# VectorE's exponential: an addition and a product as one scalar-tensor-tensor instruction

## The chip, the cores and the metric

One core of one Trainium2 chip. The metric is the device time of one execution in microseconds (us). The kernel before takes 2081.48 us, the median of three runs (2080.36 to 2085.64).

## The reference

Four residual layers on a sequence of 2048 tokens with 512 features, 32 heads of 16 each. Layers 0 and 2 are of kind A, layers 1 and 3 of kind B.

```python
# A: attention within each of 4 segments of 512 tokens, plus a memory M, z of the segments before
logits = einsum(q, k) * scale + mask          # mask: causal, within the segment
a_dot = softmax(logits) @ v
a_mem = (phi(q) @ M) / (phi(q) @ z + 1e-6)    # phi(t) = t + 1 where t > 0, else exp(t)
o = g * a_mem + (1 - g) * a_dot               # g = sigmoid(beta), per head
M, z = M + phi(k)^T v, z + sum(phi(k))
# B: full attention, 2048 x 2048 for each head, no mask
p = softmax(einsum(q, k) * Dh ** -0.5)
o = p @ v
# the program
x = x + A(layernorm(x)); x = x + B(layernorm(x)); x = x + A(layernorm(x)); x = x + B(layernorm(x))
```

The bulk of the work is the exponential of the scores: in each B layer 32 x 2048 x 2048 of them.

## The kernel before

**Banks and rounds.** Scores are made in pieces called banks: for one head, 128 keys on the partitions and up to 512 queries along the free dimension, which fills one of PSUM's eight banks with fp32. A group is one head and 512 queries; in a B layer it mostly has 64 banks (16 blocks of keys in each of four rows of TensorE). The program goes in rounds (`unit`). In each round TensorE (PE) makes three banks of scores into PSUM banks 0 to 2 or, every other round, 3 to 5. Then ScalarE (ACT) takes the exponential of all three in one instruction, 128 x 1536, PSUM to the SBUF tile `pT` (L1168). Two rounds later (three for A) PE multiplies `pT` with the values `VB` and adds it up in PSUM bank 6, which holds the group that is being summed. When a group ends, `finish` has VectorE (DVE) transpose that bank into `tT` (L1228) and take the reciprocal of the sums (L1232); GpSimd (POOL) multiplies the two (L1243). PE's first product of the next group waits for that transpose.

**The second exponential.** DVE takes some banks off ACT. `dx_pick` decides in each round whether one more bank of a B group is made, into PSUM bank 7; it looks at how far DVE is behind in the planner's account, at the time when bank 7 comes free, and at how many banks the group has given already. `dx_first` has DVE read the bank at once (L850): it scales it by a constant and writes it as a fixed-point number, 32 bits, into one of four buffers (`dxt` 0 and 1, later also the places of `KA` and `QA`). The upper 16 bits are the whole part of the exponent, the lower 16 the fraction. Two banks make a pair of 128 x 1024; sometimes a bank goes alone, 128 x 512. `dx_chain` then takes a pair through six instructions, each a step of its own: the fraction as an f16 `f` (L876), a first polynomial step `z` (L879), a product (L882), an addition (L884), a product (L886), and at last the whole part times 128 plus `z`, as an int16 whose bits are the bf16 result (L888). `f` and the result lie in one of five output buffers (`dxo`, and a part of `VA`), `z` in `dxz` or a part of `VA`. Two chains (`task_dx`) run at a time, and their steps alternate. PE multiplies the result with `VB` like any `pT`, at the earliest two rounds after the last step was put in (`dxq`).

**The order.** All instructions are put in order beforehand, by a planner that is part of the program: `Sched` keeps an estimated clock for each engine from the `ns` of each instruction (an instruction behind a busy engine adds `ns` less 85), and derives the semaphore waits. Each engine runs its instructions strictly in that order. Besides the attention there are background tasks: layer norms, projections, the memory of A, the output products, and the two chains. After every round `credit` gives a task budget for DVE (`cr_dve`, 1560 a round once all buffers are in use), and `background` runs steps as long as the budget covers the third value of a step's `yield`, the charge. `c` are the charges and `ns` the durations of the chain: 350, 610, 1150 and 690, 430, 1225 for a pair. Where `late("dve")`, DVE's clock less PE's, is over a limit, no step is run and no bank is taken. `keep_busy` adds products of zeros on PE until a round has a set number of columns.

The banks that A and B read and the tasks' needs decide which rounds count as low (few banks are ready); then no bank is taken.

Of the kernel before, what the change touches and what calls it, by code (L numbers as in the profile page):

```python
# [5 lines left out]
ALU = mybir.AluOpType  # L6
# [13 lines left out]
EXP_C1, EXP_C2, EXP_C3 = 128 * 0.69511679, 128 * 0.22764497, 128 * 0.07706706  # L20
# [222 lines left out]
class Builder:  # L243
# [621 lines left out]
    def dx_chain(self, k, b, ents, slot):  # L865


        w = 512 * len(ents)
        ns = (690, 430, 1225) if len(ents) == 2 else (420, 295, 690)
        half = self.dx_space("in", b).bitcast(dt.uint16).rearrange("p (n two) -> p two n", two=2)  # L870
        lo, hi = half[:, 0, 0:w], half[:, 1, 0:w]
        out = self.dx_space("out", slot)
        f, z, ob = out.bitcast(dt.float16)[:, 0:w], self.dx_space("z", k)[:, 0:w], out.bitcast(dt.int16)[:, 0:w]
        bt, bo, bz = self.b_dxt[b], [self.b_dxo[slot]], [self.b_dxz[k]]
        c = (350, 610, 1150) if self.wide else (440, 710, 1230)
        self.op("dve", lambda e: e.tensor_scalar(f, lo, 2.0 ** -16, None, op0=ALU.mult), reads=bt,  # L876
                writes=self.dx_writes("out", slot, self.b_dxo[slot]), ns=ns[0])
        yield [], 0, c[0]
        self.op("dve", lambda e: e.tensor_scalar(z, f, EXP_C3, EXP_C2, op0=ALU.mult, op1=ALU.add), reads=bo,  # L879
                writes=self.dx_writes("z", k, self.b_dxz[k]), ns=ns[1])  # L880
        yield [], 0, c[1]
        self.op("dve", lambda e: e.tensor_tensor(z, z, f, ALU.mult), reads=bo + bz, writes=bz, ns=ns[0])  # L882
        yield [], 0, c[0]
        self.op("dve", lambda e: e.tensor_scalar(z, z, EXP_C1, None, op0=ALU.add), reads=bz, writes=bz, ns=ns[1])  # L884
        yield [], 0, c[1]
        self.op("dve", lambda e: e.tensor_tensor(z, z, f, ALU.mult), reads=bo + bz, writes=bz, ns=ns[0])  # L886
        yield [], 0, c[2]
        self.op("dve", lambda e: e.scalar_tensor_tensor(ob, hi, 128.0, z, op0=ALU.mult, op1=ALU.add), reads=bt + bz, writes=bo, ns=ns[2])  # L888
        self.dx_bufs.append(b)
        self.dx_now[k] = []  # L890
        self.dx_use[slot] = len(ents)
        for i, (g, what, r) in enumerate(ents):
            self.dxq.append((self.step + 2, g, what, r, slot, i))
# [523 lines left out]
```

## Time and profile before

| | us |
|---|---|
| median of three runs | 2081.48 |
| the profiled execution | 2084.59 |
| its span | 2082.9 |
| ACT, all exponentials of scores (L1168), 1569 instructions | 1962.5 |
| DVE, first step of the taken banks (L850), 428 instructions | 291.2 |
| DVE, additions of the chain (L884) of 1024 | 86.8 |
| DVE, products of the chain (L886) of 1024 | 140.8 |
| DVE, last steps (L888) of 1024 | 247.3 |

The profiled execution is one run with the hardware profiler on. Its span runs from the first instruction to the last; 1.7 us of its time lie around it. PE is TensorE's products, PEld its weight loads, SP the queue that starts the transfers. A group's line gives the source line, the engine, the operation, the tile written and the tiles read, the shapes, the number of instructions, then the busy time, the mean duration of one in ns, and the idle time of the engine just before. Neighbours on DVE overlap, so the sum of durations is above the busy time of the engine. The TensorE clock granted was 0.978 of full speed.

### The profile page before, as it was taken

How to read it: one execution, taken by the hardware profiler on the slowest of the kernel's cores; microseconds unless marked ns; L12 is line 12 of the kernel's file. 1: busy time of each engine (PE TensorE's matmuls, PEld its weight loads, DVE VectorE, ACT ScalarE, POOL GpSimd, SP SyncE). 2: the span in 40 equal slices, each digit the busy share in tenths (PEclk: the TensorE clock that was granted, in tenths of full speed). 3: DMA queues.
4: the chain of work that ended last, by engine and by line, in shares of the span. 5: the costliest groups of instructions: out<-in, count | busy, mean ns of one | idle time of the engine just before them, and what ended most of it. 6: DMA issues, size and time to landing. Idle time of an engine off the chain costs nothing.

```text
span 2082.9 us, 35052 instructions
## 1 busy us (share of the span) xinstructions
PE 1787.6 (86%) x13708; PEld 494.1 (24%) x13708; DVE 1656.6 (80%) x3039; ACT 1990.0 (96%) x1610; POOL 383.9 (18%) x766
## 2 busy tenths in 40 slices
PE   7888899878988988889888888888888888888887
PEld 3222222222222222222222222222222222222222
DVE  6665655499568895898858986549999999999996
ACT  7788998999999999999999999999999999999998
POOL 4521433020060001500024001401100000000000
PEclk9898999999999999999999999999999999999999
DMA  4111100000000000000000001000000000000000
GB/s 143 21 21 21 20 5 19 11 1 14 9 1 11 1 14 9 11 11 1 14 16 4 1 1 21 11 11 1 11 1 1 1 11 1 1 1 11 1 1 11
DMA packets 67142, 24.81 MB, mean 12 GB/s; under 512 B 59808, under 2 KB 66464, under 8 KB 66976
## 3 DMA queue, kind: packets, MB, share of 16 engines
q1 hardware_dynamic: 66976, 22.57, 4.9%
q8 instruction: 107, 1.75, 0.4%
q14 instruction: 59, 0.48, 0.1%
HBM read 6.30 MB, written 2.10 MB: 4 GB/s over the span
## 4 chain that ended last, share of the span: by engine, by line
ACT 41%; PE 20%; DVE 19%; issue 15%; POOL 1%; DMA 1%; SPq 1%; ACTq 0%; DVEq 0%
ACT pT L1168 41%; PE ps L372 20%; DVE dxo L888 2%; DVE tT L1228 2%; DVE dxt L850 1%; POOL pT L1183 1%; DVE dxo L876 1%; DVE KA L850 1%; DVE x L769 1%; DVE VA L882 1%; DVE QA L850 1%; DVE dxz L886 1%; DVE dxz L882 1%; DVE VB L388 1%; DVE KB L388 1%
## 5 line engine op out<-in xcount | busy, mean ns | idle before, releaser
L1168 ACT ACTIVATE pT<-ps 128x1536 bf16<-128x1536 f32 (+2 forms) x1569 | 1962.5, 1511 | 66.1 <-PE ps L372 54.1
L372 PE MATMUL ps<-qm,KB 32*128 32x512 bf16 x4096 | 507.1, 386 | 174.5 <-ACT pT L1168 164.3
L372 PE MATMUL ps<-wB,zero 128*17 128x512 bf16 x2072 | 632.8, 388 | 0.0
L372 PE MATMUL ps<-pT,VB 128*17 128x512 bf16 x3668 | 495.7, 387 | 23.4 <-DVE tT L1228 14.5
L1243 POOL TENSOR_TENSOR ob<-tT,rd 128x256 bf16<-128x256 f32 x127 | 92.4, 727 | 1143.6 <-DVE rd L1232 1112.6
L372 PEld LDWEIGHTS ps<-qm,KB 32*128 32x128 bf16 x4096 | 126.1, 91 | 708.2 <-ACT pT L1168 616.6
L1183 POOL TENSOR_SCALAR_AFFINE_SELECT pT<-pT 128x384 bf16<-128x384 bf16 (+2 forms) x512 | 210.5, 427 | 332.8 <-ACT pT L1168 323.2
L372 PEld LDWEIGHTS ps<-wB,zero 128*17 128x17 bf16 x2072 | 177.6, 92 | 112.8 <-issue 6.6
L372 PEld LDWEIGHTS ps<-pT,VB 128*17 128x17 bf16 x3668 | 114.3, 87 | 354.5 <-issue 299.5
L850 DVE TENSOR_SCALAR dxt<-ps 128x512 uint32<-128x512 f32 x213 | 145.1, 681 | 20.7 <-PE ps L372 19.7
L1228 DVE STREAM_TRANSPOSE tT<-ps 128x512 f32<-128x512 f32 x112 | 79.6, 710 | 66.5 <-PE ps L372 64.7
L372 PE MATMUL ps<-qm,KA 32*128 32x384 bf16 (+3 forms) x1024 | 104.6, 318 | 30.1 <-ACT pT L1168 27.3
L372 PE MATMUL ps<-dxo,VB 128*17 128x512 bf16 x343 | 130.0, 386 | 0.1
L372 PE MATMUL ps<-pT,VA 128*17 128x384 bf16 (+3 forms) x1024 | 103.5, 321 | 20.4 <-DVE tT L1228 14.3
L1086 POOL TENSOR_SCALAR qm<-QB,par 128x512 bf16<-128x512 bf16 x84 | 79.9, 958 | 192.5 <-PE ps L372 190.6
L372 PE MATMUL ps<-xT,wB 128*128 128x512 bf16 x256 | 73.2, 390 | 10.8 <-DVE KB L388 3.0
L850 DVE TENSOR_SCALAR KA<-ps 128x512 uint32<-128x512 f32 x109 | 74.1, 680 | 8.2 <-PE ps L372 7.7
L850 DVE TENSOR_SCALAR QA<-ps 128x512 uint32<-128x512 f32 x106 | 72.0, 680 | 4.2 <-PE ps L372 4.0
L372 PE MATMUL ps<-xT,wA 128*128 128x512 bf16 x256 | 70.4, 385 | 5.2 <-DVE xT L525 0.9
L769 DVE TENSOR_TENSOR x<-x,ps 128x512 bf16<-128x512 bf16 x60 | 41.2, 687 | 39.7 <-PE ps L372 39.6
L886 DVE TENSOR_TENSOR dxz<-dxz,dxo 128x1024 f16<-128x1024 f16 (+1 forms) x91 | 62.0, 681 | 0.7
L876 DVE TENSOR_SCALAR dxo<-dxt 128x1024 f16<-128x1024 uint16 (+1 forms) x91 | 61.0, 672 | 1.0
(128 smaller groups left out, 1706.6 us busy)
## 6 DMA issues: line engine op xcount, KB each, us to landing
out_dram<-x SPq DMA_DIRECT2D x8, 256.0 KB, 2.1
x<-in_A_x_dram SPq DMA_DIRECT2D x3, 512.0 KB, 11.0
wB<-in_B_wqkv_dram SPq DMA_DIRECT2D x1, 1536.0 KB, 13.1
xT<-xn SPq DMA_TRANSPOSE x60, 2.5
x<-in_A_x_dram SPq DMA_DIRECT2D x4, 128.0 KB, 2.2
wA<-in_A_wk_dram SPq DMA_DIRECT2D x1, 512.0 KB, 4.2
wA<-in_A_wq_dram SPq DMA_DIRECT2D x1, 512.0 KB, 5.2
wA<-in_A_wv_dram SPq DMA_DIRECT2D x1, 512.0 KB, 6.1
```

What stands on the lines that cost most here:

```text
L372: self.sc.add("pe", lambda e: e.matmul(out, lhsT, rhs, start=start, stop=stop, skip_group_check=True), reads=reads, banks=[(bank, "w", all ...
L388: self.op("dve", lambda e: e.tensor_copy(dst, src), writes=bdst, bank=bank, alloc=al, ns=690)
L769: self.op("dve", (lambda t, o: lambda e: e.tensor_tensor(self.x[:, t, :], self.x[:, t, :], o, ALU.add))(t, o), reads=[self.b_x[t]], writes ...
L850: self.op("dve", lambda e: e.tensor_scalar(d, o, SCALE * LOG2E * 65536, 127.0 * 65536, op0=ALU.mult, op1=ALU.add), writes=self.dx_writes(" ...
L876: self.op("dve", lambda e: e.tensor_scalar(f, lo, 2.0 ** -16, None, op0=ALU.mult), reads=bt, writes=self.dx_writes("out", slot, self.b_dxo ...
L882: self.op("dve", lambda e: e.tensor_tensor(z, z, f, ALU.mult), reads=bo + bz, writes=bz, ns=ns[0])
L886: self.op("dve", lambda e: e.tensor_tensor(z, z, f, ALU.mult), reads=bo + bz, writes=bz, ns=ns[0])
L1086: self.op(eng, (lambda m, q, col: lambda e: e.tensor_scalar(m, q, col, 0.0, op0=ALU.mult, op1=ALU.add))(m, q, col), reads=[bq, self.b_par] ...
L1168: self.sc.add("act", (lambda dst, src: lambda e: e.activation(dst, src, ACT.Exp, scale=SCALE))(dst, src), writes=self.b_pT[slot * 3 + i:sl ...
L1183: self.op("pool", (lambda blk, pat: lambda e: e.affine_select(blk, blk, pattern=pat, compare_op=ALU.is_ge, fill=0.0, base=0, channel_multi ...
L1228: self.op("dve", lambda e: e.transpose(tT.rearrange("p a b -> p (a b)"), src), reads=bsrc, writes=[bt], bank=bk, alloc=al, ns=710, gap=700)
L1243: self.op(eng, lambda e: e.tensor_tensor(ob, tT[:, :, 0:16], rb, ALU.mult), reads=[bt, br], writes=[self.b_ob[oi][g.e]], ns=620)
```

## The change

In `dx_chain` the addition of `EXP_C1` and the product with `f` that follows it become one instruction that computes `(z + EXP_C1) * f`. The step in between, with its charge, goes as well. The merged instruction stands behind the charge of the addition's step, `c[0]`, and is entered with the duration of the product, `ns[0]`. The sum is no longer rounded to f16 between the two.

```diff
         yield [], 0, c[1]
         self.op("dve", lambda e: e.tensor_tensor(z, z, f, ALU.mult), reads=bo + bz, writes=bz, ns=ns[0])
         yield [], 0, c[0]
-        self.op("dve", lambda e: e.tensor_scalar(z, z, EXP_C1, None, op0=ALU.add), reads=bz, writes=bz, ns=ns[1])
-        yield [], 0, c[1]
-        self.op("dve", lambda e: e.tensor_tensor(z, z, f, ALU.mult), reads=bo + bz, writes=bz, ns=ns[0])
+        self.op("dve", lambda e: e.scalar_tensor_tensor(z, z, EXP_C1, f, op0=ALU.add, op1=ALU.mult), reads=bo + bz, writes=bz, ns=ns[0])
         yield [], 0, c[2]
         self.op("dve", lambda e: e.scalar_tensor_tensor(ob, hi, 128.0, z, op0=ALU.mult, op1=ALU.add), reads=bt + bz, writes=bo, ns=ns[2])
```

The line numbers behind it move up by two: L888 of the kernel before is L886 in the changed one, L1168 is L1166, L1228 is L1226. The merged instruction is L884.

## The prediction

> **What bounds the kernel now.** I read the page's busy times first, then its slices, then a cut of the span into stretches, then the waits and VectorE's timeline inside the stretch where two engines are full.
>
> The page, parts 1 and 2:
>
> ```profile
> PE 1787.6 (86%) x13708; PEld 494.1 (24%) x13708; DVE 1656.6 (80%) x3039; ACT 1990.0 (96%) x1610; POOL 383.9 (18%) x766
> ...
> DVE  6665655499568895898858986549999999999996
> ACT  7788998999999999999999999999999999999998
> ```
>
> ScalarE (ACT) is the bound on average. VectorE's 80% is two different things: half busy in some slices, nine tenths or more from slice 28 on. That end is where a change of VectorE work can be felt. By engine and stretch (busy us and counts for PE, weight loads, DVE, ACT, POOL):
>
> ```profile
> 416.00:1384.00 968.00, 843.62 (x6514) 235.48 (x6514) 759.13 (x1396) 945.77 (x763) 184.30 (x369) 0.98 0.04 9
> 1384.00:1464.00 80.00, 68.94 (x510) 17.64 (x508) 66.94 (x123) 78.58 (x60) 11.14 (x11) 0.98 0.00 1
> 1464.00:2025.00 561.00, 474.89 (x3708) 122.18 (x3709) 546.97 (x906) 557.91 (x417) 45.79 (x47) 0.99 0.01 4
> 2025.00:2083.00 58.00, 45.35 (x337) 12.12 (x335) 40.22 (x68) 50.86 (x40) 2.14 (x2) 0.99 0.03 10
> ```
>
> From 1464 to 2025 ACT is busy 557.9 of 561 us and DVE 547.0: both are full, ACT by 3 us more. DVE has 14 us left there, and 13 us in the 80 before. Waits in that stretch show how DVE reaches ACT: PE stops for a transpose or for the read of a score bank.
>
> ```profile
> PEld ps L372 <- DVE tT L1228: 13.6, 21, 1.2
> PE ps L372 <- DVE tT L1228: 7.3, 14, 0.9
> ...
> PEld ps L372 <- DVE dxt L850: 3.6, 8, 0.9
> ...
> ACT pT L1168 <- PE ps L372: 3.1, 7, 0.8
> ```
>
> PE's stops are mostly absorbed: only 3.1 us come through to ACT. Queues run in order, so a PE that waits for DVE holds the next scores, and behind them ACT.
>
> **The change, part by part.** The groups of the three kinds of instruction, and a piece of DVE's timeline:
>
> ```profile
> L884 DVE TENSOR_SCALAR dxz<-dxz 128x1024 f16<-128x1024 f16 x102 | 44.4, 435 | 0.8
> L886 DVE TENSOR_TENSOR dxz<-dxz,dxo 128x1024 f16<-128x1024 f16 x83 | 58.3, 703 | 0.6
> L888 DVE SCALAR_TENSOR_TENSOR dxo<-KA,dxz 128x1024 int16<-128x1024 uint16 x42 | 51.0, 1214 | 0.1
> ```
>
> ```profile
> 1724.32 0.41 DVE L884 TENSOR_SCALAR VA<-VA 128x1024 f16<-128x1024 f16 x1
> 1724.66 0.68 DVE L886 TENSOR_TENSOR dxz<-dxz,dxo 128x1024 f16<-128x1024 f16 x1
> 1725.26 0.68 DVE L850 TENSOR_SCALAR KA<-ps 128x512 uint32<-128x512 f32 x1
> ...
> 1728.35 1.22 DVE L888 SCALAR_TENSOR_TENSOR VA<-dxt,VA 128x1024 int16<-128x1024 uint16 x1
> 1729.49 0.69 DVE L876 TENSOR_SCALAR dxo<-KA 128x1024 f16<-128x1024 uint16 x1
> ```
>
> Neighbours overlap by some 80 ns, so what an instruction costs a full engine is its distance to the next start: 0.34 us for the add (1724.32 to 1724.66), 0.60 for the product and for L850, 1.14 for the scalar-tensor-tensor (1728.35 to 1729.49). These are also the medians over all such rows with no idle behind them; for 512 elements they are 0.21, 0.34 and 0.60.
>
> *Price of the new instruction.* No row has it (all operands f16 and contiguous). Nearest rows: L886, same operands, 0.60; L888, same operation, 1.14, but one operand strided and integer. I take 1.14: L886 multiplies the same kind of data in half the time, so it is the kind of operation that L888 shares, and the stride alone need not slow it (L876 reads the same strided halves in 0.69). [...]
>
> So a pair of banks loses 0.34 + 0.60 = 0.94 us and gains 1.14: **+0.20 us**. A lone bank: 0.21 + 0.34 = 0.55 against 0.60, +0.05.
>
> *Counts, from the order of the built programs.* Adds and products were 203 of 1024 and 22 of 512; merged ones are 202 and 27. 202 x 1.14 + 27 x 0.60 - 203 x 0.94 - 22 x 0.55 = +43.6 us. Three more banks are taken off ACT (428 to 431): 3 x 0.60 = 1.8. One pair chain fewer and five lone ones more change the other four steps by 5 x 1.49 - 2.68 = +4.8; two L1221 and one L388 go, -2.0. DVE: **+48 us**, 1656.6 to 1705.
>
> *What the planner makes of it.* It now charges 350 credits for a step that takes 1140 ns where it charged 350 + 610 for 940, and books 605 ns on its DVE clock (690 less 85). So it believes DVE about 0.53 us earlier per pair than it is: its limits on lateness hold too late, and it puts steps in denser. ACT loses one round of three banks (1.33 us) and takes one eviction more (0.6): -0.7. No DMA or its order on SP changes; POOL has the same 770 instructions.
>
> *Where the 48 us lie.* I cut both orders after the same numbers of rounds (one round: three banks, one exponential on ACT).
>
> - Rounds 0 to 240: nothing. No bank is taken there.
> - Rounds 960 to 1440, in the profile 1384 to 2025: banks taken 229 to 234, merged instructions 109 + 16 for 109 + 6 pairs of them before. By the medians DVE's work goes from 607.0 to 641.8 us: 109 x 0.20 = 21.8, ten more lone chains at 2.09 = 20.9, five L850 3.0, less 11 us of other steps planned elsewhere. The trace has 613.9 (66.94 + 546.97), so after it is 613.9 + 34.8 = **648.7**, on 641 us. This cannot be hidden: 7.7 us is the least, if DVE never waits. It now waits 27 us; if it still waits as long, +35. Being late it will wait less for data: I take half of the dense stretch's rate, 641 x 14/561 / 2 = 8: **+15.7**.
> - Rounds 240 to 900, some 416 to 1290 us: +20.3 us in 880. DVE is 78% busy there, so the mean hides it, and ACT's exponentials are the cover. In the slices with a 9 (5 of the 19 from 8 to 26) the cover is gone: 20.3 x 5/19 = **+5.3**, bounds 0 and 20.3.
> - The rest: 900 to 960 and the tail, -2 and -5 us on DVE that is idle there anyway: 0.
>
> Sum: 15.7 + 5.3 - 0.7 = **+20.3**. The profiled execution took 2084.6 (span 2082.9 and 1.7 around it), so 2104.9 there; it lies 3.1 above the median of 2081.5, so I predict 2102. With all bounds: +7 to +54.6, 2088 to 2136.
>
> What is late next: L850 and the transposes L1228 behind a merged instruction; PE waits for both, then ACT for PE.
>
> **The rivals.**
>
> 1. *It is hidden.* Four input and five output buffers let DVE fall behind where it is full and catch up in the 18 us that it idles after 2025. For: of 21 us of PE stops for L1228 only 3.1 reach ACT. Against: one score bank (7) and one accumulator (6) pass through DVE, so it can be late by a round or two, not by 8 us. Gain of ACT's lost round kept, up to 6 us lost: 2081 to 2087.
> 2. *Not slower: the merged instruction runs at L886's rate.* In the dense stretch each pair then costs 0.60 for 0.94: 641.8 - 109 x 0.54 = 583 us, under ACT's 641. It decides wherever the price lies below 0.94. ACT stays the bound, so at most ACT's idle of the dense stretch (4.5), a little of the 22 us of 416 to 1384, and 0.7 come back: 2074 to 2080, say 2077.
> 3. *Half rate.* No row has two contiguous f16 inputs with a constant between them, so none excludes a slower form. As a mechanism of this kernel: twice L888's distance, 2.28, so 109 x 1.14 = 124 us more in the dense stretch alone, and about 40 in the bursts before: 2265. Against it: L888 has two inputs that are not bf16 either, and its 1.21 us for 1024 is twice L886's, not four times. [...]
> 4. *Lateness multiplies.* Planned by a wrong clock, PE meets late output buffers (L888 to its product) beside late banks, and then DVE waits for PE in its turn: twice my middle, +41 and more, 2123 to 2150.
> 5. *The new order packs better.* Eleven rounds fewer count as low between 900 and 1020, so banks are taken sooner (21 to 29 in 960 to 1020). Worth at most ACT's idle there, a few us beyond rival 1: about 2074.
>
> **How the numbers follow.** A measurement can tell 0.3%, 6.2 us, from no change: 2075.2 to 2087.7. Forecast (2088 to 2122) 0.60; hidden 0.12; L886's rate 0.09 (0.04 of it under 2075); half rate 0.04; multiplied 0.10; packing 0.05, all faster. Slower 0.60 + 0.04 + 0.10 = 0.74; same 0.12 + 0.05 = 0.17; faster 0.09. The range 2079 to 2131 leaves out the half rate, most of the packing, the lower part of rival 2 and most of 4: about 0.2.
>
> **What would show it.** Right: a row of L884 with two inputs at about 1.21 us and 1.14 to the next start; DVE over 98% in 1384 to 2045; waits of PE for L850 and L1228 grown, and of ACT for PE from 3 us to some 15. Wrong: L884 at 0.69 (rival 2) or above 2 (rival 3); DVE full and ACT's waits unchanged (rival 1); PE waiting long for L888 (rival 4). If the extra time lies before 1384, my sharing of the 20 us was wrong.

## The result and the profile after

The changed kernel takes 2181.77 us, the median of four runs (2179.03 to 2185.52), against 2081.93 for the kernel before in the same comparison: 1.0478 of it, 95% interval 1.0455 to 1.0501. Its profiled execution has a span of 2183.8 us, 100.9 more than the 2082.9 of before. I had predicted 2102, 20 us more.

Both spans cut at the first exponentials of rounds 240, 900, 960, 1020 and 1440, by the view of busy times in stretches (us, then busy us and counts of PE, weight loads, DVE, ACT, POOL, then the granted clock of PE). The prediction had placed these rounds 3 to 30 us later. Before:

```profile
386.00:1287.00 901.00, 784.17 (x6053) 217.27 (x6050) 723.90 (x1324) 882.98 (x708) 158.49 (x309) 0.98 0.04 8
1287.00:1369.00 82.00, 73.47 (x570) 21.47 (x569) 45.70 (x94) 78.72 (x68) 26.50 (x61) 0.98 0.06 13
1369.00:1455.00 86.00, 74.27 (x534) 19.49 (x529) 63.42 (x116) 82.42 (x62) 10.38 (x11) 0.98 0.01 2
1455.00:2022.00 567.00, 479.29 (x3747) 123.18 (x3744) 552.97 (x915) 563.91 (x420) 47.94 (x49) 0.99 0.01 4
```

After:

```profile
385.00:1325.00 940.00, 789.80 (x6009) 219.28 (x6058) 747.57 (x1223) 889.75 (x706) 161.43 (x310) 0.96 0.04 8
1325.00:1412.00 87.00, 78.30 (x566) 22.14 (x573) 42.45 (x86) 79.65 (x71) 25.53 (x63) 0.94 0.06 13
1412.00:1496.00 84.00, 70.22 (x522) 18.28 (x519) 79.82 (x142) 80.87 (x61) 13.15 (x12) 0.96 0.00 1
1496.00:2119.00 623.00, 525.17 (x3745) 132.33 (x3749) 590.34 (x808) 572.34 (x422) 44.40 (x46) 0.93 0.01 3
```

The 420 rounds of the dense stretch (1020 to 1440) take 56 us more, rounds 240 to 900 take 39 more; all the rest together 6. In the dense stretch DVE is busy 37 us more, but the time grows by 56: DVE idles more than before (33 us for 14), and so does ACT (51 for 3). In rounds 240 to 900 DVE idles 192 us of 940, and the time grows all the same. PE's granted clock is lower in both (0.93 for 0.99 in the dense stretch, 0.96 for 0.98 in the other).

The waits within the dense stretch, before and after (who waited for whom, us, times, the longest):

```profile
...
PEld ps L372 <- DVE tT L1228: 13.6, 21, 1.2
PE ps L372 <- DVE tT L1228: 7.3, 14, 0.9
...
PEld ps L372 <- DVE dxt L850: 3.6, 8, 0.9
ACT pT L1168 <- PE ps L372: 3.1, 7, 0.8
```

```profile
...
ACT pT L1166 <- PE ps L372: 49.9, 59, 2.7
PEld ps L372 <- DVE tT L1226: 34.6, 21, 2.9
...
PE ps L372 <- DVE tT L1226: 28.0, 20, 2.6
PEld ps L372 <- DVE dxt L850: 26.3, 38, 1.9
PEld ps L372 <- DVE KA L850: 15.7, 24, 1.7
PE ps L372 <- DVE dxt L850: 15.5, 25, 1.6
```

PE stops for the same two things as before, the transposes of a finished group and the reading of bank 7, but the longest stop for a transpose is 2.9 us where it was 1.2. And it is passed on: ACT waits 49.9 us for PE, 3.1 before.

The merged instruction itself, from the groups of instructions:

```profile
L884 DVE SCALAR_TENSOR_TENSOR VA<-VA,dxo 128x1024 f16<-128x1024 f16 x83 | 103.3, 1245 | 1.4
L884 DVE SCALAR_TENSOR_TENSOR VA<-VA 128x1024 f16<-128x1024 f16 x18 | 22.0, 1221 | 0.4
```

About 1.22 us, as L888 before (1.21 to 1.24): here the same price for two f16 operands as for an integer and an f16 one. One stop, in the timeline of after:

```profile
1795.15 0.69 DVE L882 TENSOR_TENSOR dxz<-dxz,dxo 128x1024 f16<-128x1024 f16 x1
1795.88 1.23 DVE L884 SCALAR_TENSOR_TENSOR dxz<-dxz,dxo 128x1024 f16<-128x1024 f16 x1
...
1796.04 0.39 PE L372 MATMUL ps<-qm,KB 32*128 32x512 bf16 x3 [0.63 <-ACT pT L1166]
1797.03 0.68 DVE L850 TENSOR_SCALAR dxt<-ps 128x512 uint32<-128x512 f32 x1
1797.63 0.71 DVE L1226 STREAM_TRANSPOSE tT<-ps 128x512 f32<-128x512 f32 x1
1798.37 0.25 DVE L1230 RECIPROCAL rd<-tT 128x16 f32<-128x16 f32 x1
...
1798.39 0.60 PE L372 MATMUL ps<-pT,VB 128*17 128x512 bf16 x5 [1.95 <-DVE tT L1226]
...
1799.46 0.61 PE L372 MATMUL ps<-qm,KB 32*128 32x512 bf16 x4
...
1800.01 1.02 PE L372 MATMUL ps<-wB,zero 128*17 128x512 bf16 x2
...
1800.17 1.45 ACT L1166 ACTIVATE pT<-ps 128x1536 bf16<-128x1536 f32 x1 [1.50 <-PE ps L372]
```

DVE runs L882, L884 and L850 and only then comes to the transpose; PE idles 1.95 us for it. The five products behind it still take 0.38 us each (the row's 0.60 is for all five). From 1799.2 to 1802.6 PE's clock is halved, and its mean from 1798 to 1802 is 0.65: the four products at 1799.46 take 0.60 us each where the same had taken 0.38 at 1794.70, and the two of zeros at 1800.01 span 1.02 us where two had spanned 0.59 at 1793.90. The next exponential starts 1.50 us late.

### The profile page after: what moved, and what is told of

It reads as the page before. It is cut to its first block, busy times and chain, and to the rows that moved or that the text cites. A ratio compares the mean times of both kernels' runs of the same rounds, so it can differ in the third digit from the quotient of the medians.

```text
span 2183.8 us, 34706 instructions
## 1 busy us (share of the span) xinstructions
PE 1833.8 (84%) x13603; PEld 504.7 (23%) x13704; DVE 1730.3 (79%) x2834; ACT 2003.4 (92%) x1610; POOL 384.5 (18%) x766
## 4 chain that ended last, share of the span: by engine, by line
DVE 53%; PE 26%; ACT 11%; issue 7%; DMA 1%; POOL 1%; SPq 1%; ACTq 0%; DVEq 0%
PE ps L372 26%; ACT pT L1166 10%; DVE dxo L886 7%; DVE VA L884 5%; DVE dxt L850 5%; DVE dxz L884 5%; DVE dxo L876 4%; DVE VA L882 3%; DVE dxz L882 3%; DVE QA L850 3%; DVE tT L1226 2%; DVE KA L850 2%; DVE VA L886 2%; DVE dxz L879 2%; DVE VA L879 1%
## 5 line engine op out<-in xcount | busy, mean ns | idle before, releaser
L1166 ACT ACTIVATE pT<-ps 128x1536 bf16<-128x1536 f32 (+2 forms) x1568 | 1974.4, 1388 | 152.7 <-PE ps L372 140.4
L372 PE MATMUL ps<-qm,KB 32*128 32x512 bf16 x4096 | 551.0, 397 | 143.7 <-ACT pT L1166 104.2
L372 PE MATMUL ps<-wB,zero 128*17 128x512 bf16 x2068 | 658.1, 402 | 0.0
L372 PE MATMUL ps<-pT,VB 128*17 128x512 bf16 x3665 | 507.3, 397 | 68.7 <-DVE tT L1226 50.3
L372 PEld LDWEIGHTS ps<-qm,KB 32*128 32x128 bf16 x4096 | 134.6, 91 | 710.6 <-ACT pT L1166 474.2
L1181 POOL TENSOR_SCALAR_AFFINE_SELECT pT<-pT 128x256 bf16<-128x256 bf16 (+2 forms) x512 | 210.6, 427 | 340.1 <-ACT pT L1166 330.7
L850 DVE TENSOR_SCALAR dxt<-ps 128x512 uint32<-128x512 f32 x216 | 147.3, 682 | 34.3 <-PE ps L372 33.6
L1226 DVE STREAM_TRANSPOSE tT<-ps 128x512 f32<-128x512 f32 x112 | 79.5, 710 | 81.3 <-PE ps L372 81.1
L372 PE MATMUL ps<-qm,KA 32*128 32x512 bf16 (+3 forms) x1024 | 105.1, 318 | 29.5 <-ACT pT L1166 26.2
L372 PE MATMUL ps<-pT,VA 128*17 128x512 bf16 (+3 forms) x1024 | 102.7, 321 | 21.9 <-DVE tT L1226 15.7
L884 DVE SCALAR_TENSOR_TENSOR VA<-VA,dxo 128x1024 f16<-128x1024 f16 (+1 forms) x96 | 112.6, 1173 | 1.5
L884 DVE SCALAR_TENSOR_TENSOR dxz<-dxz,dxo 128x1024 f16<-128x1024 f16 (+1 forms) x89 | 104.0, 1168 | 1.6
L850 DVE TENSOR_SCALAR KA<-ps 128x512 uint32<-128x512 f32 x108 | 73.4, 680 | 12.6 <-PE ps L372 12.5
L850 DVE TENSOR_SCALAR QA<-ps 128x512 uint32<-128x512 f32 x107 | 73.1, 683 | 6.4 <-PE ps L372 6.1
```

Of the source, the lines that this page charges most:

```text
L372: self.sc.add("pe", lambda e: e.matmul(out, lhsT, rhs, start=start, stop=stop, skip_group_check=True), reads=reads, banks=[(bank, "w", all ...
L850: self.op("dve", lambda e: e.tensor_scalar(d, o, SCALE * LOG2E * 65536, 127.0 * 65536, op0=ALU.mult, op1=ALU.add), writes=self.dx_writes(" ...
L884: self.op("dve", lambda e: e.scalar_tensor_tensor(z, z, EXP_C1, f, op0=ALU.add, op1=ALU.mult), reads=bo + bz, writes=bz, ns=ns[0])
L1166: self.sc.add("act", (lambda dst, src: lambda e: e.activation(dst, src, ACT.Exp, scale=SCALE))(dst, src), writes=self.b_pT[slot * 3 + i:sl ...
L1181: self.op("pool", (lambda blk, pat: lambda e: e.affine_select(blk, blk, pattern=pat, compare_op=ALU.is_ge, fill=0.0, base=0, channel_multi ...
L1226: self.op("dve", lambda e: e.transpose(tT.rearrange("p a b -> p (a b)"), src), reads=bsrc, writes=[bt], bank=bk, alloc=al, ns=710, gap=700)
```

## The experiments

A round's order and its instructions can be separated, because the planner writes the order beforehand. "Dense" is the length of rounds 1020 to 1440. A planner's clock is called true or false here as the durations booked on it for DVE are; "PE clock" is the one granted to TensorE. "Neighbours" counts, in these rounds, the chain steps that stand right behind the instruction that they wait for, mostly the step before in their own chain, for the first step the reading of the bank (68 of the 276 in after). All ratios are to the kernel before on the same chip, with their 95% intervals.

| | banks | neighbours | dense, us | PE clock, whole | us | ratio |
|---|---|---|---|---|---|---|
| before | 428 | 31 | 568 | 0.978 | 2081.93 | 1 |
| after | 431 | 276 | 623 | 0.949 | 2181.77 | 1.0478 (1.0455 to 1.0501) |
| e1: order of after, two instructions | 431 | 382 | 610 | 0.959 | 2171.54 | 1.0417 (1.0396 to 1.0439) |
| e2: order of before, merged | 428 | 59 | 595 | 0.967 | 2120.68 | 1.0172 (1.0153 to 1.0191) |
| e3: after, true clock and charge | 409 | 98 | 574 | 0.972 | 2110.22 | 1.0126 (1.0104 to 1.0149) |
| e4: after, true clock | 418 | 65 | 571 | 0.972 | 2104.85 | 1.0092 (1.0070 to 1.0115) |
| e5: after, true charge | 439 | 86 | 617 | 0.955 | 2175.44 | 1.0434 (1.0400 to 1.0467) |
| e6: before, false clock | 440 | 86 | 592 | 0.963 | 2151.07 | 1.0326 (1.0297 to 1.0354) |
| e7: before, one chain at a time | 410 | 345 | 583 | 0.967 | 2118.75 | 1.0178 (1.0145 to 1.0212) |
| e9: after, fewer banks | 403 | 219 | 604 | 0.955 | 2180.69 | 1.0456 (1.0436 to 1.0476) |
| e10: before, no zeros | 408 | 224 | 571 | 0.700 | 2136.13 | 1.0235 (1.0210 to 1.0260) |
| e13: after, no zeros | 415 | 327 | 602 | 0.682 | 2205.28 | 1.0592 (1.0556 to 1.0629) |
| e14: after, half the zeros | 415 | 293 | 609 | 0.891 | 2173.04 | 1.0430 (1.0385 to 1.0474) |
| e15: before, half the zeros | 410 | 238 | 574 | 0.920 | 2103.84 | 1.0097 (1.0067 to 1.0126) |

**Instructions or order (e1, e2).** e1 keeps the order of after and splits the merged instruction; the odd bookings leave the planner's clock as it was.

```diff
-        self.op("dve", lambda e: e.scalar_tensor_tensor(z, z, EXP_C1, f, op0=ALU.add, op1=ALU.mult), ..., ns=ns[0])
+        self.op("dve", lambda e: e.tensor_scalar(z, z, EXP_C1, None, op0=ALU.add), ..., ns=0, gap=-85)
+        self.op("dve", lambda e: e.tensor_tensor(z, z, f, ALU.mult), ..., ns=ns[0] - 35, gap=ns[0] - 85)
```

> The order of the changed kernel, instruction for instruction, with the addition and the product as two instructions one behind the other in place of the merged one; the planner's clock and charges are those of the changed kernel. Theory P (price: the merged instruction costs 0.2 us more than the two, and VectorE was full): the cause is taken away, so within 0.5% of the kernel before, 2075 to 2092 us. Theory O (order: charged 350 and booked 605 ns, the planner runs one chain at a time and no longer knows how late VectorE is, so each step waits for the one before): the cause is still there, over 2140 us, and VectorE's busy time in rounds 1020 to 1440 stays above 575 us (554 before, 590 after). Between 2092 and 2140: both have a part. In either theory the time at half clock of TensorE in that stretch (7 us before, 82 after) follows the time.

e2 is the reverse: the addition is booked and charged, but not put in.

```diff
-        self.op("dve", lambda e: e.tensor_scalar(z, z, EXP_C1, None, op0=ALU.add), reads=bz, writes=bz, ns=ns[1])
+        booked = Op("dve", 0, None)
+        booked.deps = [bz[0].last_write]
+        self.sc.estimate(booked, ns[1], ns[1] - 85, None)
+        bz[0].last_write.end = booked.end
         yield [], 0, c[1]
-        self.op("dve", lambda e: e.tensor_tensor(z, z, f, ALU.mult), ...)
+        self.op("dve", lambda e: e.scalar_tensor_tensor(z, z, EXP_C1, f, op0=ALU.add, op1=ALU.mult), ...)
```

> The order of the kernel before, with the addition left out of the program but booked and charged as before, and the merged instruction where the product stood. Theory P: the price is paid in full, 2160 to 2185 us. Theory O: only the price of 0.2 us a pair is paid and the chains still alternate, so what my prediction's sum gave, 2090 to 2110 us, with VectorE's busy time in rounds 1020 to 1440 at about 554 + 21 = 575 us.

The order alone costs 88 us (2171.54 less 2083.53, the kernel before in that comparison), the instruction in the old order 37; both together cost 100, so they overlap. Theory O holds, P falls as the main cause. The 88 are not free of the instruction's form: 106 of e1's 382 neighbours are the product behind its own addition. And e2 is above the 2090 to 2110 of my sum. Its order was planned with 0.95 us for what takes 1.14, so DVE is later than planned by 0.19 us a pair there too; its 37 us are not the price of the work alone. DVE's work in its dense stretch is as reckoned (554 + 21 = 575 was expected):

```profile
1466.00:2061.00 595.00, 502.34 (x3743) 128.53 (x3749) 575.11 (x812) 569.14 (x421) 49.56 (x49) 0.96 0.01 4
```

The stretch grew by 28 us for 22 of work, and the clock fell with it, from 0.99 to 0.96.

**What in the order (e3 to e7, e9).** Two entries are false in after: the charge and the booked duration. e3 mends both, e4 the duration alone, e5 the charge alone.

```diff
-        yield [], 0, c[0]
-        self.op("dve", lambda e: e.scalar_tensor_tensor(...), ..., ns=ns[0])
+        yield [], 0, c[0] + c[1]          # e3, e5
+        self.op("dve", lambda e: e.scalar_tensor_tensor(...), ..., ns=ns[2])          # e3, e4
```

> The changed kernel with the merged instruction booked with the duration of the last step (1225 ns) and charged as the two steps were (c[0] + c[1]). 409 banks are taken, 22 fewer than in the changed kernel, so ScalarE has some seven rounds more, +9 us. Theory O: the chains alternate again and the lateness is known, 2085 to 2110 us. Theory P: the price is still there but fewer banks are taken, 2130 to 2170 us.

> The changed kernel with only the booked duration mended (1225 ns), the charge left at c[0]; 418 banks taken. Neighbouring steps of one chain in rounds 1020 to 1440 fall from 276 to 65. Theory O: like the run with both mended, 2085 to 2110 us. If the charge is what matters instead, as slow as the changed kernel, over 2150 us. Theory P: 2140 to 2175 us.

> The changed kernel with only the charge mended (c[0] + c[1]), the merged instruction still booked as 605 ns where it takes 1140; 439 banks taken, and neighbouring steps of one chain in rounds 1020 to 1440 fall from 276 to 86. What is in the order? Theory C (clock: the planner does not know how late VectorE is): still slow, over 2140 us. Theory N (neighbours: steps that wait for the step just before cost VectorE some 0.1 us each): as fast as the mended kernels or the merged instruction in the old order, 2100 to 2125 us.

The booked duration is what matters: e4, with one number changed in the source, takes 77 us off the changed kernel, e5 takes off 6. e3 is just above what was expected, e4 within it. In e4's dense stretch (1466 to 2037 us) the stops are nearly back to those of before, and ACT's wait for PE with them:

```profile
PEld ps L372 <- DVE tT L1226: 17.2, 21, 1.8
...
ACT pT L1166 <- PE ps L372: 5.2, 10, 1.0
```

In e5 the chains alternate again (86 neighbours), DVE's clock is still false, and it is as slow as after. e6 puts a false clock into the kernel before, without the merged instruction:

```diff
-        self.op("dve", lambda e: e.tensor_scalar(z, z, EXP_C1, None, op0=ALU.add), reads=bz, writes=bz, ns=ns[1])
+        self.op("dve", lambda e: e.tensor_scalar(z, z, EXP_C1, None, op0=ALU.add), reads=bz, writes=bz, ns=0, gap=-85)
```

> The kernel before, two instructions and all charges kept, but the addition booked with no time, so that the planner's clock for VectorE falls 0.34 us short for each pair; 440 banks taken, 86 neighbouring steps in rounds 1020 to 1440. Theory C: slower than before by a good part of what the order costs, 2110 to 2160 us. Theory N: no cost but 12 more banks off ScalarE, 2070 to 2092 us.

`gap=-85` takes 85 ns off the planner's clock each time that DVE is busy, so this clock falls some 0.42 us a pair short, not the 0.34 that I expected. The kernel takes 67 us more than before, with the same instructions, the same charges and 12 more banks off ACT. The theory of neighbours had 2070 to 2092 and falls as the cause here. e7 tests it by itself:

```diff
-        ready = [t for t in self.dx_tasks[:1 + self.wide] if self.met(t["next"][0])]
+        ready = [t for t in self.dx_tasks[:1] if self.met(t["next"][0])]
```

> The kernel before with one chain at a time in place of two: in rounds 1020 to 1440 345 steps of 593 stand behind the step that they wait for (31 of 630 before), but all bookings and charges are true; 410 banks taken, 18 fewer, which gives ScalarE six rounds more, +8 us. Theory N: VectorE loses some 0.09 us at each of 314 neighbours, 28 us, in a full stretch, and the time is over 2115 us. Theory C: 2086 to 2100 us.

2118.75 us: 35 more, 8 of which are ACT's six rounds. So one chain at a time does cost, some 27 us, in a kernel whose clock is true. It is above what the theory of the clock alone allowed (2086 to 2100). But a kernel with few neighbours and a false clock (e5) is as slow as after. Against e1, which books 0.34 us a pair too little and has 382 neighbours, e6 books 0.42 too little and has 86: 67 us for e1's 88. So some 20 us of the 88, or more, go with the neighbours and the charge, near e7's 27, and the rest with the clock. The two runs also differ by nine banks, so this split is rough.

By the error of the booking, the time above the kernel before is 21 us where there is none (e4), 37 at 0.19 us a pair (e2), 67 at 0.42 (e6), 91 and 100 at 0.53 (e5 and after); the instructions, banks and neighbours of these kernels differ as well.

e9 asks if a false clock costs because it lets DVE be given too much:

```diff
-    ALT3, ALT5, GAP, AHEAD, PE_B, PE_A, PE_LOW, LOW, PAIRS, TAKEN, PAIRS2 = 3, 5, 2, 250, 3, 2, 6, 24, 60, 5, 0
+    ALT3, ALT5, GAP, AHEAD, PE_B, PE_A, PE_LOW, LOW, PAIRS, TAKEN, PAIRS2 = 3, 5, 2, 250, 3, 2, 6, 24, 60, 8, 0
```

> The changed kernel with at most an eighth of a group's banks given to VectorE in place of a fifth: 403 banks, 28 fewer, booked and charged as falsely as before. By the distances of the profile before, VectorE's work in rounds 1020 to 1440 is now 498 us, under the 547 of the kernel before, on ScalarE's 561. Does the false clock cost time because it lets VectorE be overloaded, or because single readings of banks are planned for a time at which VectorE isn't there? Overload: nothing is left but nine rounds more on ScalarE, 12 us, so 2090 to 2115 us. Misplaced: the lateness in bursts stays, over 2130 us, with 30 us and more at half clock in these rounds.

Its dense stretch:

```profile
1504.00:2108.00 604.00, 503.06 (x3694) 128.64 (x3697) 522.74 (x717) 569.12 (x421) 39.30 (x47) 0.95 0.01 4
```

and its waits there:

```profile
ACT pT L1166 <- PE ps L372: 34.6, 41, 3.1
PEld ps L372 <- DVE tT L1226: 32.5, 21, 3.5
```

DVE is busy 523 of 604 us; it idles 81, six times as long as in the kernel before, and the kernel is as slow as after. The stretch is 19 us shorter than in after, and the nine rounds more cost 12; so the amount has a small part, but 36 us over the kernel before remain. What stops PE is a transpose or a reading of bank 7 that the planner placed for a moment at which DVE is still busy with instructions that it booked too short. Which of the planner's uses of the clock does most of it (the limit for bank 7, or those for the steps) was not tried.

**Why it costs more than the stop (e10, e13 to e15).** e10 takes the products of zeros out of the kernel before, `BUSY_COLS = 0` for 1024; e13 does so in after; e14 and e15 have 512.

> The kernel before without the products of zeros that keep TensorE busy; 408 banks, so seven rounds more, +9 us; no other engine's work changes. If the granted clock follows TensorE's idle time and a halved clock is what stretches the rounds (1.77 us where they start at half clock, 1.33 else), the mean clock falls from 0.978 to under 0.9, and the time is over 2130 us although TensorE has 630 us less to do. If the clock follows something else, it stays about 0.97, and the time is 2085 to 2100 us.

The clock falls to 0.70, and the time grows by 50 us (2136.13 against 2086.54 for the kernel before in that comparison), with nothing added to any engine but seven rounds. In these kernels the clock falls with what PE is given to do: 0.978 with all the zeros, 0.920 with half of them (e15), 0.700 with none. But the second half of my reasoning is not borne out where I had put it: in the dense stretch PE is at half clock for most of the time (482 us of it, a mean of 0.58), and the stretch is hardly longer than before (571 us for 568).

```profile
1487.00:2058.00 571.00, 484.10 (x2960) 91.65 (x2963) 543.07 (x874) 566.87 (x422) 45.13 (x47) 0.58 0.01 4
```

So without the zeros the work of these 420 rounds still fits at that clock. The loss lies in the earlier rounds (0 to 900: 32 us more), where projections and output products are in the queue too, and behind round 1440, where the seven rounds were added (some 10 us). That a halved clock hurts where PE has more to do than fits into a round is how I read it; no run shows it by itself.

> The changed kernel without the products of zeros; 415 banks, false clock as before. In the kernel before without them TensorE ran at half clock for 482 us of rounds 1020 to 1440 and these rounds still took 570 us, since there is little for it to do. So if what the false clock costs there (623 - 568 = 55 us) is the stop of TensorE alone, these rounds stay near 600 us and over; if most of it is the queue of zeros at half clock behind a stop, they come to 570 to 585 us, and the whole time to 2136 + 10 to 40 us.

> The changed kernel with half the products of zeros; 415 banks. Between the two: if a stop costs by the zeros that run at half clock behind it, rounds 1020 to 1440 take less than the 623 us of the changed kernel, 585 to 605; if it is the stop alone, 610 and over.

> The kernel before with half the products of zeros, the partner of the run above; 410 banks, 18 fewer, +8 us. Clock between 0.70 and 0.978; rounds 1020 to 1440 between 567 and 575 us, the whole 2090 to 2135 us.

```profile
1530.00:2132.00 602.00, 521.28 (x2957) 99.85 (x2960) 572.77 (x781) 570.67 (x421) 45.00 (x47) 0.55 0.01 3
```

e13's dense stretch takes 602 us, as expected if the stop alone costs the time, and its whole is 69 us above e10, where 10 to 40 were expected if it was mostly the zeros. With no zeros, the false clock costs 602.4 - 570.5 = 32 us in the dense stretch; with half of them 609 - 574 = 35; with all 623 - 568 = 55. More than half of it is thus there without any zeros, and some 23 us come with them; that they run at half clock behind a stop is the likely reason, not one that was tested by itself. e14's 609 us lies between the two ranges that I had given it, and e15 came out within its own. The three pairs differ by some banks as well, so the split is rough.

**A chain with less work (e8, e11, e12).** If DVE's time is what is scarce, the addition and the product should go, not be merged. A polynomial of second degree has neither:

```diff
-        self.op("dve", lambda e: e.tensor_scalar(z, f, EXP_C3, EXP_C2, op0=ALU.mult, op1=ALU.add), ...)
+        self.op("dve", lambda e: e.tensor_scalar(z, f, 128 * 0.3398, 128 * 0.6602, op0=ALU.mult, op1=ALU.add), ...)
         yield [], 0, c[1]
         self.op("dve", lambda e: e.tensor_tensor(z, z, f, ALU.mult), reads=bo + bz, writes=bz, ns=ns[0])
-        yield [], 0, c[0]
-        self.op("dve", lambda e: e.tensor_scalar(z, z, EXP_C1, None, op0=ALU.add), ...)
-        yield [], 0, c[1]
-        self.op("dve", lambda e: e.tensor_tensor(z, z, f, ALU.mult), ...)
         yield [], 0, c[2]
```

Its largest relative error is 0.27%, for the banks that DVE takes.

> The kernel before with a polynomial of second degree in place of the third, so one product and one addition fewer in each chain, 0.94 us a pair, and nothing merged; booking and charges of the steps left as they are. 465 banks taken, 37 more, 12 rounds fewer on ScalarE. If VectorE's full stretch is what the time hangs on, 0.94 us less a pair must pay: at ScalarE's floor 12 x 1.33 = 16 us less, 2060 to 2075 us. If the 244 neighbouring steps of one chain in rounds 1020 to 1440 cost more than that gives, 2080 us and over.

> The kernel with the polynomial of second degree, and up to a quarter of a group's banks given to VectorE, to the 30th before the end: 473 banks, 45 more than the kernel before, 15 rounds fewer, 20 us less for ScalarE. The clock is true, so lateness is known: 2062 to 2078 us. If it is over 2083, the share of VectorE was already the best one.

> The kernel with the polynomial of second degree, and a bank is also taken when bank 7 comes free 600 ns late by the planner's clock, not 300: 472 banks, and 145 neighbours of one chain in rounds 1020 to 1440 in place of 244. If known lateness of 0.3 us is absorbed, 2060 to 2078 us; if TensorE's stops for bank 7 reach ScalarE, over 2080.

e8 takes 2079.44 us, ratio 0.9973 (0.9958 to 0.9987), between its two ranges, just under the upper one: DVE has 46 us to spare in the dense stretch, and 12 rounds fewer bring 16 us, but rounds 240 to 900 grew by 18. e11 (up to a quarter of a group, `REST` 30 and `TAKEN` 4) takes 2076.18, 0.9949 (0.9931 to 0.9967); e12 (`DX_BANK` 600) 2075.98, 0.9951 (0.9936 to 0.9966). Both are half a per cent faster than the kernel before, and within what was expected.

## Why the prediction was wrong, step by step

**Price of the merged instruction: right.** 1.14 us from start to start, taken from L888; the rows of after have 1.22 us for one, as L888's 1.21, and 1.15 from L884 to the next start in the timeline above. The rivals of L886's rate and of half rate are out.

**The sum for DVE: right for the instruction, short for the order.** I had 0.20 us a pair; e2 has +22 us of DVE work in the dense stretch for 104 pairs, which is that. But for rounds 960 to 1440 I had +34.8, and it was 670.2 - 616.4 = +53.8 by the stretches above. The rest came with the order. With both entries false the planner mostly runs one chain after the other (276 neighbours; 65 and 86 with one of the two mended), and a product whose successor waits for it takes 0.72 or 0.73 us to the next start where others take 0.60 or 0.61, in the traces of before and after alike. I had counted the instructions of the new order, but not looked at which stand next to each other.

**"This cannot be hidden": not what the rows say.** I had cut the profile at 1384 to 2025 for rounds 960 to 1440, which in fact lie from 1369 to 2022. There DVE is busy 616.4 of 653 us and idles 36.6, not 27, so with my +34.8 it would have had 651.2 us to do. The least was nothing, not 7.7 us.

**"What the planner makes of it": the step that failed.** I wrote that its limits on lateness hold too late, and gave this no price in the sum. It is most of the result: with the booked duration mended and nothing else, the changed kernel takes 2104.85 us, so the false clock is 77 of the 100 us. That 2104.85 is near my 2102 is partly luck: e4 takes 13 banks fewer off ACT, and its time lies elsewhere than I had put it (rounds 960 to 1440 without growth, 653 us as before, where I had +15.7). I treated lateness as an amount (DVE's work against ACT's in a stretch), and e9 shows that it is one of moments: with 81 us of idle DVE the stops remain.

**The share of rounds 240 to 900: failed for the same reason.** I gave them 5.3 us because DVE idles there, with the slices at nine tenths as the measure. They took 39 more, with 192 us of idle DVE. With the booked duration mended (e4) they took 9 more, so most of the 39 is the false clock's: a late instruction in an idle stretch stops PE just as well.

**"Being late it will wait less for data": wrong.** I let 8 us of DVE's idle time stay. By the stretches above it idles 36.6 us in rounds 960 to 1440 before and 36.8 after: 18 us that it had to spare in rounds 960 to 1020 are filled, and in the dense stretch it idles 19 us more, while PE, stopped and for 82 us at half clock, delivers later (DVE's readings of bank 7, L850, wait 14.6 us for PE in after, 2.7 before). So the whole of the 53.8 us of new work comes out as time (707 - 653 = 54). This was rival 4, "lateness multiplies", at 2123 to 2150 and 0.10. Late banks, and DVE that waits for PE in its turn, are in the traces; the late output buffers that it also named are not (0.2 us of PE's waits in the dense stretch). I had priced it as twice my middle, and not seen that the clock takes part: PE's granted clock stands in every window of the profile, 0.98 to 1.00 in the dense stretch, and I read it as a constant.

**Rival 1, hidden, and rival 5, packing: out.** Rounds 960 to 1020 took 84 us for 86, and the one round fewer is there, but that is all. The 21 us of PE stops for L1228 that rival 1 leaned on count largely the same stops twice, once at the products (7.3) and once at their weight loads (13.6).

## What to carry to other kernels

In a program whose order is planned from entered durations, such a duration is part of the change: when an instruction is replaced, enter the measured time of the new form, and price a wrong entry as a change of the order, not as a change of work. Before merging two instructions, compare their distances to the next start with that of the merged form: here 0.34 + 0.60 us against 1.14. And where one queue waits for single moments of another, spare time on average is no cover; look at the longest stop of each wait (1.2 us before, 2.9 after) beside its sum.

## What the runs showed of the hardware

In the traces of before and after, the granted clock of PE has shares of 1.0 and 0.5 alone. In the dense stretch the half came in pieces of 3.4 or 6.8 us, with PE busy some 84% over the stretch in both: 7 us in 2 pieces before, 82 us in 17 pieces after. In the 3.4 us ahead of each of the 17, PE was busy 19 to 75% of the time, 54% in the median, and its longest single stop lasted 0.6 to 2.1 us; ahead of the one at 1799 us it was the stop of 1.95 us above, with PE busy 35% of that time. At a mean clock of 0.58 in the dense stretch, without the zeros (e10), the rounds took no more than 3 us longer.
